# Linear attention feeding a mixture of experts: the rows of x prepared three blocks ahead, with four transposed buffers

## The chip, the cores and the metric

The kernel runs on one core of a Trainium2 chip. The metric is the time of one execution on the device in microseconds (us); lower is better. A run's time is a little longer than the span of its profile, which goes from the first to the last instruction that the profile shows.

## The reference, cut to what matters

```
q_s = softmax(q, axis=-1);  k_s = softmax(k, axis=2)            # q, k, v: 8 x 8 x 576 x 64
kv  = einsum('bhsd,bhse->bhde', k_s, v)
x   = einsum('bhsd,bhde->bhse', q_s, kv)  -> rows of 512         # 8 x 576 = 4608 rows
for b, s:
    fresh_e = argmax(x[b, s] @ w_gate)                           # 8 experts
    e = fresh_e if s == 0 or sigmoid(x[b, s] @ w_local) < 0.5 else prev_e
    p = softmax(x[b, s] @ w_gate)
    out[b, s] = p[e] * (relu(x[b, s] @ w1[e]) @ w2[e])           # w1: 512 x 1024, w2: 1024 x 512
```

Each of the 4608 rows of x goes to one expert, and which one hangs on the rows before it in its sequence.

## The kernel before, in words

The first part (up to about 150 us) works out the attention and writes the rows of x, not yet divided by their sums, to a buffer `xrows` in device memory. The rows are then sorted by expert into blocks of 128 rows, at most 43 of them (`NBM`), and each block is a pass through the two layers of one expert.

A block needs its rows prepared, in steps that stand on different engines:

- `gather` (line 828, POOL) fetches the 128 rows into one of four buffers `xg`.
- `prep_x` (`Px`, line 839, POOL, a few on VectorE) scales them by their sums into one of two buffers `xn`.
- `prep_hi` (`Ph`, line 184, ACT) writes the upper half of a split into two float16 numbers, and `prep_lo` (`Pl`, line 847, VectorE) the lower half, into one of two buffers `x2`. The trace calls these `x`.
- `turn_dma` (`D`, line 860, issued by SyncE) transposes both halves by DMA into one of three buffers `xT`.

Then TensorE runs `ffn1` (lines 882 and 887, half of the hidden units at a time, accumulators `ph` and `pi`); `act_copy`, `act_add`, `act_hi`, `act_lo` (lines 892, 895, 898, 902) add the two parts on ACT and VectorE, apply the relu and split the result into `hi` and `lo`; `ffn2` (line 909) multiplies by the second layer into the accumulator `py`; `give` (line 912, ACT) scales it by the row's share into one of two buffers `y`; and `put` (line 916, POOL) stores the rows by an indirect DMA. Since the stores go to rows that only the data name, each waits for the one before it.

All weights are split into float16 pairs too. `fetch` (line 976, SyncE, 2 MB each for w1 and for w2, into `s1` and `s2`) loads the next expert's weights, on a condition that is read at run time; `renew` (lines 184 and 938, ACT and VectorE) cuts them into `w1h`, `w1l`, `w2h`, `w2l` where a block begins a new expert.

Each engine works through its own list in order. For the first part and blocks 0 to 5 the order is a list written by hand, `ORDER`; a name such as `Px.6` is a step and a block. From block 6 on the order is that of the function `block(b)`:

```
        if b + AHEAD < NBM:
            gather(b + AHEAD)
        prep_a(b + 2)
        ...
        prep_b(b + 2)
        act(b, 1)
        ...
        ffn2(b, 0)
        ...
        if b + 2 < NBM:
            turn_dma(b + 2)
        fetch(b, 2)
        if b + 1 < NBM:
            fetch(b + 1, 1)
```

`prep_a` is `prep_x`, `prep_b` is `prep_hi` and `prep_lo`. TensorE's order in `block(b)` is `ffn1(b, 0)`, `ffn2(b - 1, 1)`, `ffn1(b, 1)`, `ffn2(b, 0)`. `AHEAD` is 4. Blocks 36 and up run only if the data need them. A block that is at most half full runs `ffn1` on 64 rows, so it is shorter.

Of the kernel before, what the change touches and what calls it, by code (L numbers as in the profile page):

```python
# [9 lines left out]
F16 = mybir.dt.float16  # L10
F32 = mybir.dt.float32
# [12 lines left out]
P = 128  # L24
# [117 lines left out]
bo.2 bo.0 Ar.3.0 bo.1 RN.3.3 Al.3.0 Gv.2 s2.3 bm.1 xs.3.2 bo.3 bm.0 Ac.3.1 ro.2.8 F2.3.0 ro.3.8 RN.4.1 Ad.3.1 Pt.2 ro.3.1 ro.3.6 bi.p0 F1.4.0 ro.3.7  # L142
Ar.3.1 s1.4 bi Sd.1 RN.4.2 Al.3.1 bj.p0 ro.3.3 F2.3.1 bj.p1 Ac.4.0 bj.p2 RN.5.0 ro.2.5 Ad.4.0 bm.3 Gv.3 bj.p3 bm.2 F1.4.1 Ar.4.0 bx.p0 RN.4.3 Al.4.0
bx bj.p4 F2.4.0 G.6 Ac.4.1 RN.5.1 Ad.4.1 G.7 Ar.4.1 bj F1.5.0 Al.4.1 s1.5 G.8 Gp.6 F2.4.1 Ac.5.0 Px.6 RN.6.0 Px.7 Ad.5.0 Ph.6 Ar.5.0 Pl.6 Ph.7 Al.5.0
F1.5.1 D.6 Gv.4 Pl.7 Pt.4 D.7 Pt.3 s2.4 RN.5.2 RN.5.3 F2.5.0 RN.6.1 s2.5 Ac.5.1 s1.6 G.9 Ad.5.1 Ar.5.1 Al.5.1
"""


# [1 line left out]
def moe_kernel(ctx, tc, q, k, v, w_gate, w_local, w1, w2, out, dbg=None):  # L150
# [433 lines left out]
    def r_o(t, c):  # L584

        o_ = oo[:, t * NCH + c, :]
        if on("ro", t, c) is nc.vector:
            nc.vector.tensor_scalar(out=o_, in0=iot1, scalar1=off[:, t, c:c + 1], scalar2=val[:, c:c + 1],
                                    op0=ALU.is_equal, op1=ALU.mult)
        else:  # L590
            da = sp.tile([P, P], F32, name="da")
            nc.scalar.activation(da, iot1, AF.Abs, bias=off[:, t, c:c + 1], scale=-1.0)
            nc.scalar.activation(o_, da, AF.Relu, bias=val[:, c:c + 1], scale=nval[:, c:c + 1])

# [195 lines left out]
    def open_w():  # L790

        ck.close()
        wp = ctx.enter_context(tc.tile_pool(name="wp", bufs=1, side="right"))
        for n, sh, dt in (("s1", [P, 4, DF], F32), ("s2", [P, 8, DM], F32), ("w1h", [P, 4, DF], F16),
                          ("w1l", [P, 4, DF], F16), ("w2h", [P, 8, DM], F16), ("w2l", [P, 8, DM], F16)):
            W[n] = wp.tile(sh, dt, name=n)
        fp = ctx.enter_context(tc.tile_pool(name="fp", bufs=1, side="right"))
        pst = ctx.enter_context(tc.tile_pool(name="pst", bufs=1, space=PSUM, side="right"))
        psy = ctx.enter_context(tc.tile_pool(name="psy", bufs=1, space=PSUM, side="right"))
        turns(fp, xg, AHEAD, [P, ROW], F32, "xg")  # L800
        turns(fp, xn, 2, [P, DM], F32, "xn")
        turns(fp, x2, 2, [P, 2, DM], F16, "x2")
        turns(fp, xT, 3, [P, 2, 4, P], F16, "xT")
        turns(fp, pb, NPB, [P, 1], F32, "pb")
        turns(pst, pt, 1, [P, 2, 4, P], F16, "pt")
        turns(psy, py, 1, [P, DM], F32, "py")
        psh = ctx.enter_context(tc.tile_pool(name="psh", bufs=1, space=PSUM, side="right"))
        fe = ctx.enter_context(tc.tile_pool(name="fe", bufs=1, side="right"))
        turns(fe, hi, 2, [P, 8, P], F16, "hi")
        turns(fe, lo, 2, [P, 8, P], F16, "lo")  # L810
        turns(fe, hf, 2, [P, 4, P], F32, "hf")
        turns(fe, ys, 2, [P, DM], F32, "y")
        turns(psh, ph, 1, [P, 4, 2 * P], F32, "ph")
# [40 lines left out]
                nc.tensor.transpose(pt[0][:, i, c, :], x2[b % 2][:, i, P * c:P * c + P], id16)  # L854

    def turn_copy(b):
        nc.vector.tensor_copy(out=xT[b % 3], in_=pt[0])

    def turn_dma(b):
        nc.sync.dma_start(out=xT[b % 3].rearrange("p i c t -> p (i c) t"), in_=x2[b % 2].rearrange("p i d -> p (i d)"),  # L860
                          transpose=True)

    def ffn1(b, g):
# [9 lines left out]

    def hidden(b, g, n):

        ph_, xT_ = ph[g % len(ph)], xT[b % 3]
        phs[g] = ph_
        for f in range(4):
            fs = slice(P * (4 * g + f), P * (4 * g + f) + P)

            def big(c):
                nc.tensor.matmul(ph_[:, f, :].rearrange("p (i t) -> p i t", i=2)[:, :, 0:n], W["w1h"][:, c, fs], xT_[:, :, c, 0:n],  # L882
                                 start=(c == 0), stop=(c == 3))

            big(0)
            for c in range(4):
                nc.tensor.matmul(ph_[:, f, 0:n], W["w1l"][:, c, fs], xT_[:, 0, c, 0:n], start=False, stop=False)  # L887
            for c in range(1, 4):
                big(c)
# [74 lines left out]
    def fetch(b, i):  # L964
# [8 lines left out]
        elif b == NA - 2 and i == 2:  # L973
# [2 lines left out]
        nc.sync.dma_start(out=s_, in_=src(bass.ds(word(e, NE - 1, [ET.SP]), 1)), **kw)  # L976

    pl = Plan(dict(kt=NKT, vt=NVT, km=2, mt=2, vp=2, pk=2, psq=2, px=1, pz=1, qt=NQT, qs=3, qe=4, xt=NXT, kvT=2, rs=3, cs=1,
                   qm=3, ex=2, xg=AHEAD, xn=2, x2=2, xT=3, pst=1, psh=1, psy=1, hh=2, hf=2, y=2, dl=1, pb=NPB),
              ("kt", "vt", "vp", "km", "xg", "xn", "x2", "xT", "pst", "psh", "hh", "hf", "y", "pb"), names(SWAP))  # L980
    add, split = pl.add, pl.split
    plan.append(pl)
# [86 lines left out]
    for b in range(NP + 4):  # L1069
        add(("G", b), POOL, gather, after=[("ax",) if b < NA else ("bx",)] + [("xs", t, u) for t in range(2 if b < NA else NTILE) for u in range(3)],  # L1070
            order=[("ow",)], takes=[("xg", b)])
        if b <= NP:
            add(("Gp", b), POOL, gather_share, after=[("ax",) if b < NA else ("bx",)] + [("Sd", t) for t in range(1 if b < NA else 2)],
                order=[("ow",)], takes=[("pb", b)])
        if b >= NP + 2:
            continue
        add(("Px", b), POOL, prep_x, alt=DVE, after=[("G", b)], uses=[("xg", b)], takes=[("xn", b)])
        add(("Ph", b), ACT, prep_hi, alt=DVE, after=[("Px", b)], uses=[("xn", b)], takes=[("x2", b)])
        add(("Pl", b), DVE, prep_lo, after=[("Ph", b)], uses=[("xn", b), ("x2", b)])
        if b < NT_PE:  # L1080
            add(("T", b), PE, turn, after=[("Pl", b)], takes=[("pst", b)], uses=[("x2", b)])
            add(("Tc", b), DVE, turn_copy, after=[("T", b)], uses=[("pst", b)], takes=[("xT", b)])
        else:
            add(("D", b), SP, turn_dma, after=[("Pl", b)], uses=[("x2", b)], takes=[("xT", b)])
        if b > NP:
            continue
        if b > 0:
            for i in range(2 if b == NP else 4):
                src = [("F1", b - 1, 0), ("F1", b - 1, 1), ("F2", b - 1, 0), ("F2", b - 1, 1)][i]
                add(("RN", b, i), ACT, renew4, after=[src, ("aj",) if b < NA else ("bj",)], order=[("s1" if i < 2 else "s2", b - 1)])  # L1090
            add(("s1", b), SP, lambda b: fetch(b, 1), after=[("RN", b, 1)] + ([("bj",)] if b >= NA - 1 else []))
        else:
            add(("s1", b), SP, lambda b: fetch(b, 1), after=[("Wl", i) for i in range(8)] + [("aj",)], order=[("W", 3)])
        if b == NP:
            continue
        add(("s2", b), SP, lambda b: fetch(b, 2),
            after=([("RN", b, 3)] if b else [("Wl", i) for i in range(8, 16)] + [("aj",)]) + ([("bj",)] if b >= NA - 2 else []))
        for g in range(2):
            wp_ = [("Wl", 4 * g + i) for i in range(4)] if b == 0 else [("RN", b, g)]
            add(("F1", b, g), PE, ffn1, after=[("Tc" if b < NT_PE else "D", b)] + wp_, order=[("ow",)] + ([("F2", b - 1, g)] if b else [("F1", 0, 0)] * g)  # L1100
                + ([("F1", b, 0)] if g else []), takes=[("psh", (b, g))], uses=[("xT", b)])
            add(("Ac", b, g), ACT, act_copy, after=[("F1", b, g)], uses=[("psh", (b, g))], takes=[("hf", (b, g))])
            add(("Ad", b, g), DVE, act_add, after=[("Ac", b, g)], uses=[("psh", (b, g)), ("hf", (b, g))])
            add(("Ar", b, g), ACT, act_hi, after=[("Ad", b, g)], uses=[("hf", (b, g))] + ([("hh", b)] if g else []), takes=[] if g else [("hh", b)])
            add(("Al", b, g), DVE, act_lo, after=[("Ar", b, g)], uses=[("hf", (b, g)), ("hh", b)])
            if b == NP - 1 and g:
                continue
            wp_ = [("Wl", 8 + 4 * g + i) for i in range(4)] if b == 0 else [("RN", b, 2 + g)]
            add(("F2", b, g), PE, ffn2, after=[("Al", b, g)] + wp_, order=[("F1", b, 1)] if g == 0 else [("F1", b + 1, 0)],
                takes=[] if g else [("psy", b)], uses=[("hh", b)] + ([("psy", b)] if g else []))  # L1110
        if b < NP - 1:
            add(("Gv", b), ACT, give, after=[("F2", b, 1), ("Gp", b)], uses=[("psy", b), ("pb", b)], takes=[("y", b)])
            add(("Pt", b), POOL, put, after=[("Gv", b)], uses=[("y", b)])
# [21 lines left out]
    def block(b):  # L1135


        if b + AHEAD < NBM:
            gather(b + AHEAD)
        prep_a(b + 2)  # L1140
        if b + 1 < NBM:
            gather_share(b + 1)
            if b + 1 not in fst:
# [8 lines left out]
        put(b - 1)  # L1152
        renew(b, FROM[b][1])
        next_(b, (2, 3))
        prep_b(b + 2)
        act(b, 1)
        renew(b, FROM[b][2])
        next_(b, (4, 5, 6, 7))
        ffn2(b, 0)
        next_(b, (8, 9))  # L1160
        if b + 2 < NBM:
            turn_dma(b + 2)
        fetch(b, 2)
        if b + 1 < NBM:
            fetch(b + 1, 1)
# [53 lines left out]
```

## Time and profile before

| what | before |
|---|---|
| median of three runs | 603.48 us (602.3, 603.48, 604.54) |
| the profiled execution's own time | 598.04 us |
| its span | 596.3 us |
| TensorE matmul busy | 516.5 us, 87% of the span |
| VectorE, ACT, POOL busy | 58%, 45%, 36% |
| mean granted clock of TensorE | 0.937 |

In a timeline row the first number is the start in us from the span's start, the second the duration; a merged row (x4) runs from the first start to the last end. A bracket names the idle time before the row and what ended it. The granted clock is a share of 2.4 GHz: 1.00 is full, 0.50 is 1.2 GHz. A row of the DMA view gives the number of issues and the median time from issue to landing.

### The profile page before, as it was taken

The numbers are of one execution on the slowest core, as the hardware profiler recorded it, in microseconds if no ns is written. First come the engines' busy times: TensorE is split into PE (matmuls) and PEld (weight loads), VectorE is DVE, ScalarE is ACT, GpSimd is POOL, SyncE is SP. The second block draws the span as 40 slices with busy tenths as digits, with TensorE's granted clock in tenths as the row PEclk, the third lists the DMA queues.
The fourth block names the chain that finished last, engine by engine and source line by source line (L and its number), as shares of the span: only waits on it lengthen the run. The fifth ranks groups of instructions, "written<-read, shape, count | busy, mean of one in ns | idle before, by whom it ended". The sixth has DMA issues, their size and how long they took to land. (4 is left out here: it accounts for less than half of the span.)

```text
span 596.3 us, 15110 instructions
## 1 busy us (share of the span) xinstructions
PE 516.5 (87%) x5558; PEld 366.1 (61%) x5558; DVE 348.8 (58%) x625; ACT 265.4 (45%) x441; POOL 213.9 (36%) x229
## 2 busy tenths in 40 slices
PE   2687966776589999799979999999999899999995
PEld 1566755554476776466656666667665666667762
DVE  3777789999978984227624853584376233333332
ACT  0534345395465533237424743564375243342432
POOL 4132323224613104623522533534434335243341
PEclk9768799777889999899989999999999999999998
DMA  9999999997855428633992596369539924333241
GB/s 238 245 240 214 259 251 263 263 211 192 287 201 143 117 83 255 241 74 96 287 128 58 158 259 85 100 199 208 111 61 286 157 58 104 68 90 83 69 103 47
DMA packets 100241, 98.29 MB, mean 165 GB/s; under 512 B 55199, under 2 KB 83871, under 8 KB 100128
## 3 DMA queue, kind: packets, MB, share of 16 engines
q1 hardware_dynamic: 92480, 74.66, 52.6%
q0 software_dynamic: 7648, 22.20, 13.4%
q8 instruction: 62, 1.02, 0.8%
q14 instruction: 51, 0.42, 0.3%
HBM read 206.76 MB, written 20.89 MB: 382 GB/s over the span
## 5 line engine op out<-in xcount | busy, mean ns | idle before, releaser
L909 PE MATMUL py<-w2h,hi 128*128 128x512 f16 x304 | 116.0, 382 | 8.2 <-ACTq L954 3.7
L916 POOL DMA_INDIRECT out<-y,sidx x38 | 39.2, 1032 | 217.8 <-ACTq L954 155.2
L909 PE MATMUL py<-w2h,lo 128*128 128x512 f16 x304 | 115.8, 381 | 0.6
L909 PE MATMUL py<-w2l,hi 128*128 128x512 f16 x304 | 115.8, 381 | 0.1
L882 PEld LDWEIGHTS <-w1h 128*128 128x128 f16 x1216 | 104.9, 99 | 14.6
L887 PEld LDWEIGHTS <-w1l 128*128 128x128 f16 x1216 | 92.3, 99 | 22.8 <-issue 6.0
L882 PE MATMUL ph<-xT,w1h 128*128 128x256 f16 (+1 forms) x624 | 99.1, 273 | 7.9 <-DMA xT<-x 7.9
L909 PEld LDWEIGHTS <-hi 128*128 128x128 f16 x608 | 58.8, 98 | 66.2 <-issue 9.7
L882 PE MATMUL pi<-xT,w1h 128*128 128x256 f16 (+1 forms) x592 | 91.7, 268 | 0.0
L902 DVE SCALAR_TENSOR_TENSOR lo<-hf,hi 128x512 f16<-128x512 f32 x76 | 56.9, 749 | 46.1 <-ACTq L954 38.9
L898 ACT ACTIVATE hi<-hf 128x512 f16<-128x512 f32 x76 | 47.8, 629 | 70.1 <-DVE hf L895 69.3
L895 DVE TENSOR_TENSOR hf<-ph,hf 128x512 f32<-128x512 f32 x39 | 26.9, 689 | 84.3 <-ACT hf L892 81.6
L892 ACT COPY hf<-ph 128x512 f32<-128x512 f32 x39 | 22.7, 582 | 97.6 <-PE ph L882 94.2
L847 DVE SCALAR_TENSOR_TENSOR x<-xn,x 128x512 f16<-128x512 f32 x40 | 33.7, 845 | 46.8 <-ACT x L184 45.7
L887 PE MATMUL ph<-xT,w1l 128*128 128x128 f16 (+1 forms) x624 | 60.5, 221 | 0.0
L887 PE MATMUL pi<-xT,w1l 128*128 128x128 f16 (+1 forms) x592 | 55.9, 217 | 0.0
L828 POOL DMA_INDIRECT xg<-xrows,gidx x42 | 44.6, 1062 | 30.2 <-issue 11.4
L909 PEld LDWEIGHTS <-lo 128*128 128x128 f16 x304 | 29.9, 98 | 39.1 <-DVE lo L902 2.5
L834 POOL DMA_INDIRECT pb<-shares,gidx x39 | 45.7, 1171 | 10.2 <-issue 6.8
L357 PE MATMUL pk<-VP,KT 128*64 128x65 f32 (+1 forms) x640 | 41.1, 286 | 4.0 <-POOL VP L186 1.9
L357 PEld LDWEIGHTS pk<-VP,KT 128*64 128x64 f32 (+1 forms) x640 | 33.5, 185 | 12.5 <-issue 4.7
L410 POOL TENSOR_TENSOR qs<-qt,qm 128x512 f32<-128x512 f32 x23 | 24.8, 1092 | 42.1 <-DVE qm L404 21.0
(223 smaller groups left out, 667.4 us busy)
## 6 DMA issues: line engine op xcount, KB each, us to landing
s<-in_moe_w SPq DMA_DIRECT2D x77, 2048.0 KB
xrows<-xt SPq DMA_DIRECT2D x12, 888.0 KB
qt<-in_q SPq DMA_DIRECT2D x24, 384.0 KB
KT<-in_k SPq DMA_DIRECT2D x16, 512.0 KB
VT<-in_v SPq DMA_DIRECT2D x16, 512.0 KB
s<-in_moe_w SPq DMA_DIRECT2D x4, 1024.0 KB
KT<-in_k SPq DMA_DIRECT2D x8, 128.0 KB
VT<-in_v SPq DMA_DIRECT2D x8, 128.0 KB
```

Of the source, the lines that this page charges most:

```text
L357: nc.tensor.matmul(pkv[64 * i:64 * i + 64, g], KT[b % NKT][ps, 4 * i + g, c], VP[b % 2][ps, 4 * i + g, c], start=(c == 0), stop=(c == KC - 1))
L410: on("qs", t, c).tensor_tensor(out=qs[t, c].rearrange("p (g x) d -> p g x d", x=2), in0=qt[t, c // 3][:, :, c % 3, :].rearrange("p (x g) d ...
L828: nc.gpsimd.indirect_dma_start(out=xg[b % AHEAD], out_offset=None, in_=src, in_offset=bass.IndirectOffsetOnAxis(ap=i_[:, j_:j_ + 1], axis=0))
L834: nc.gpsimd.indirect_dma_start(out=pb[b % NPB], out_offset=None, in_=src, in_offset=bass.IndirectOffsetOnAxis(ap=i_[:, j_:j_ + 1], axis=0))
L847: nc.vector.scalar_tensor_tensor(out=x2[b % 2][:, 1, :], in0=xn[b % 2], scalar=XS, in1=x2[b % 2][:, 0, :], op0=ALU.mult, op1=ALU.subtract)
L882: nc.tensor.matmul(ph_[:, f, :].rearrange("p (i t) -> p i t", i=2)[:, :, 0:n], W["w1h"][:, c, fs], xT_[:, :, c, 0:n], start=(c == 0), stop ...
L887: nc.tensor.matmul(ph_[:, f, 0:n], W["w1l"][:, c, fs], xT_[:, 0, c, 0:n], start=False, stop=False)
L895: nc.vector.tensor_tensor(out=hf[g], in0=phs[g][:, :, 0:P], in1=hf[g], op=ALU.add)
L898: nc.scalar.activation(hi[b % 2][:, 4 * g:4 * g + 4, :], hf[g], AF.Relu)
L902: nc.vector.scalar_tensor_tensor(out=lo[b % 2][:, gs_, :], in0=hf[g], scalar=0.0, in1=hi[b % 2][:, gs_, :], op0=ALU.max, op1=ALU.subtract)
L909: nc.tensor.matmul(py[0], h_[:, f, :], w_[:, f, :], start=(f == 0 and i == 0), stop=(f == 7 and i == 2))
L916: nc.gpsimd.indirect_dma_start(out=outr, out_offset=bass.IndirectOffsetOnAxis(ap=i_[:, j_:j_ + 1], axis=0), in_=ys[b % 2], in_offset=None, ...
```

## The change

The functions of the loop prepare block b+3 where they prepared block b+2. The transposed rows get a fourth buffer. Since the loop now starts with block 9, the preparation of block 8 (`Px.8 Ph.8 Pl.8`, `D.8`) is added to the written order. A scratch tile `da` of the sorting step goes from three buffers to two.

```diff
 bx bj.p4 F2.4.0 G.6 Ac.4.1 RN.5.1 Ad.4.1 G.7 Ar.4.1 bj F1.5.0 Al.4.1 s1.5 G.8 Gp.6 F2.4.1 Ac.5.0 Px.6 RN.6.0 Px.7 Ad.5.0 Ph.6 Ar.5.0 Pl.6 Ph.7 Al.5.0
-F1.5.1 D.6 Gv.4 Pl.7 Pt.4 D.7 Pt.3 s2.4 RN.5.2 RN.5.3 F2.5.0 RN.6.1 s2.5 Ac.5.1 s1.6 G.9 Ad.5.1 Ar.5.1 Al.5.1
+F1.5.1 D.6 Gv.4 Pl.7 Px.8 Ph.8 Pl.8 Pt.4 D.7 D.8 Pt.3 s2.4 RN.5.2 RN.5.3 F2.5.0 RN.6.1 s2.5 Ac.5.1 s1.6 G.9 Ad.5.1 Ar.5.1 Al.5.1
...
-            da = sp.tile([P, P], F32, name="da")
+            da = sp.tile([P, P], F32, name="da", bufs=2)
...
-        turns(fp, xT, 3, [P, 2, 4, P], F16, "xT")
+        turns(fp, xT, 4, [P, 2, 4, P], F16, "xT")
...
-        nc.sync.dma_start(out=xT[b % 3].rearrange("p i c t -> p (i c) t"), in_=x2[b % 2].rearrange("p i d -> p (i d)"),
+        nc.sync.dma_start(out=xT[b % 4].rearrange("p i c t -> p (i c) t"), in_=x2[b % 2].rearrange("p i d -> p (i d)"),
                           transpose=True)
...
-        ph_, xT_ = ph[g % len(ph)], xT[b % 3]
+        ph_, xT_ = ph[g % len(ph)], xT[b % 4]
...
-        if b >= NP + 2:
+        if b >= NP + 3:
             continue
...
-        prep_a(b + 2)
+        prep_a(b + 3)
...
-        prep_b(b + 2)
+        prep_b(b + 3)
         act(b, 1)
...
-        if b + 2 < NBM:
-            turn_dma(b + 2)
+        if b + 3 < NBM:
+            turn_dma(b + 3)
         fetch(b, 2)
```

How the lists of two engines change where the loop begins: POOL first. `xg` is a gather, `xn` the scaling, `pb` the gather of the shares, `out` the store. Before:

```order
L834 DMA pb_1707<-shares,gidx_76 128x1
L839 TENSOR_TENSOR xn_1699<-xg_1697 128x512
L954 UNCONDITIONAL_BRANCH
L916 DMA out<-y_1723,sidx_73 4608x512
L916 DMA out<-y_1724,sidx_73 4608x512
L828 DMA xg_1695<-xrows,gidx_76 128x592
L954 UNCONDITIONAL_BRANCH x3
L828 DMA xg_1696<-xrows,gidx_76 128x592
L839 TENSOR_TENSOR xn_1698<-xg_1694 128x512
L834 DMA pb_1708<-shares,gidx_76 128x1
```

After:

```order
L834 DMA pb_1708<-shares,gidx_76 128x1
L839 TENSOR_TENSOR xn_1699<-xg_1697 128x512
L954 UNCONDITIONAL_BRANCH
L839 TENSOR_TENSOR xn_1698<-xg_1694 128x512
L916 DMA out<-y_1724,sidx_73 4608x512
L916 DMA out<-y_1725,sidx_73 4608x512
L828 DMA xg_1695<-xrows,gidx_76 128x592
L828 DMA xg_1696<-xrows,gidx_76 128x592
L839 TENSOR_TENSOR xn_1699<-xg_1695 128x512
L834 DMA pb_1709<-shares,gidx_76 128x1
```

The fourth row of the new list is the scaling of block 8; it now stands ahead of the stores of blocks 4 and 3. Where block 8 was scaled (next to last row of the old list), block 9 is, whose gather is the one two rows above it, with one gather between.

SyncE's list at the same place, from the transpose of block 6 to the first weight fetch (`s`) behind it. Before:

```order
L860 DMA_TRANSPOSE xT_1702<-x_1700 128x8x128
L860 DMA_TRANSPOSE xT_1703<-x_1701 128x8x128
L822 TENSOR_LOAD info_74 x2
L976 REGISTER_ALU x2
L976 ISA
L976 DMA s_1680<-in_moe_w 128x8x512
```

After:

```order
L860 DMA_TRANSPOSE xT_1704<-x_1700 128x8x128
L860 DMA_TRANSPOSE xT_1705<-x_1701 128x8x128
L860 DMA_TRANSPOSE xT_1702<-x_1700 128x8x128
L822 TENSOR_LOAD info_74 x2
L976 REGISTER_ALU x2
L976 ISA
L976 DMA s_1680<-in_moe_w 128x8x512
```

The transpose of block 8 stands between that of block 7 and the weight fetch.

## Rows read from the trace of the kernel before

**Rows 1.** page, part 1: busy us (share of the span) x instructions
```profile
PE 516.5 (87%) x5558; PEld 366.1 (61%) x5558; DVE 348.8 (58%) x625; ACT 265.4 (45%) x441; POOL 213.9 (36%) x229
```

**Rows 2.** stretches: us, busy us (x) of each engine, granted clock, DMA share, GB/s
```profile
309.60:313.90 4.30, 4.28 (x32) 3.60 (x32) 0.00 (x0) 0.00 (x0) 0.00 (x0) 0.60 0.41 112
...
500.00:580.00 80.00, 80.00 (x688) 55.71 (x686) 26.99 (x39) 28.94 (x47) 32.64 (x32) 1.00 0.37 85
```

**Rows 3.** waits of TensorE: line waited for, us in total, times, longest us
```profile
PE ph L882 <- DMA xT<-x: 7.9, 4, 3.2
```

**Rows 4.** timeline of TensorE: start us, us, instruction, [idle before <-releaser]
```profile
237.55 0.27 PE L882 MATMUL ph<-xT,w1h 128*128 128x256 f16 x1
...
248.62 0.58 PE L909 MATMUL py<-w2h,hi 128*128 128x512 f16 x1 [3.04 <-ACTq L954]
...
305.99 0.38 PE L909 MATMUL py<-w2h,lo 128*128 128x512 f16 x1
309.62 0.32 PE L882 MATMUL ph<-xT,w1h 128*128 128x256 f16 x1 [3.25 <-DMA xT<-x]
...
313.91 0.38 PE L909 MATMUL py<-w2h,hi 128*128 128x512 f16 x1
...
316.50 0.27 PE L882 MATMUL pi<-xT,w1h 128*128 128x256 f16 x1
...
319.14 0.38 PE L909 MATMUL py<-w2h,hi 128*128 128x512 f16 x1
...
365.01 0.27 PE L882 MATMUL ph<-xT,w1h 128*128 128x256 f16 x1 [1.33 <-DMA xT<-x]
```

**Rows 5.** timeline of SyncE's queue, before the loop and around the longest wait
```profile
231.52 4.80 SPq L860 DMA_TRANSPOSE xT<-x  x2
238.41 13.59 SPq L976 DMA_DIRECT2D s<-in_moe_w  x3
...
286.39 2.26 SPq L860 DMA_TRANSPOSE xT<-x  x1
289.99 1.53 SPq L976 DMA_DIRECT2D s<-in_moe_w  x2
294.68 3.76 SPq L860 DMA_TRANSPOSE xT<-x  x1
...
304.77 1.27 SPq L860 DMA_TRANSPOSE xT<-x  x1
```

**Rows 6.** timeline of ACT, block 6 and around the longest wait
```profile
247.88 0.69 ACT L912 ACTIVATE y<-py,pb 128x512 f32<-128x512 f32 x1 [5.46 <-DMA xg<-xrows,gidx]
...
317.81 0.63 ACT L184 ACTIVATE x<-xn 128x512 f16<-128x512 f32 x1 [0.42 <-ACTq L954]
...
328.60 0.61 ACT L184 ACTIVATE x<-xn 128x512 f16<-128x512 f32 x1
```

**Rows 7.** DMA issues at 351.75, at 240.73, of the whole span: median us to landing
```profile
xg<-xrows,gidx POOLq DMA_INDIRECT x1, 13.0
...
out<-y,sidx POOLq DMA_INDIRECT x1, 7.1
...
out<-y,sidx POOLq DMA_INDIRECT x38, 3.1
```

**Rows 8.** timeline of POOL, before the loop and in it
```profile
232.59 1.04 POOL L839 TENSOR_TENSOR xn<-xg 128x512 f32<-128x512 f32 x1 [3.79 <-DMA xg<-xrows,gidx]
235.14 1.02 POOL L916 DMA_INDIRECT out<-y,sidx  x1 [1.52 <-ACTq L954]
240.73 1.00 POOL L916 DMA_INDIRECT out<-y,sidx  x1 [4.56 <-DMA out<-y,sidx]
...
320.03 1.06 POOL L839 TENSOR_TENSOR xn<-xg 128x512 f32<-128x512 f32 x1
...
351.75 1.02 POOL L828 DMA_INDIRECT xg<-xrows,gidx  x1 [0.30 <-issue]
...
363.14 1.06 POOL L839 TENSOR_TENSOR xn<-xg 128x512 f32<-128x512 f32 x1
```

More of the change, by code (lines that the diff above doesn't have):

```diff
@@ L856, in turn_copy @@
     def turn_copy(b):
-        nc.vector.tensor_copy(out=xT[b % 3], in_=pt[0])
+        nc.vector.tensor_copy(out=xT[b % 4], in_=pt[0])
     def turn_dma(b):
-        nc.sync.dma_start(out=xT[b % 3].rearrange("p i c t -> p (i c) t"), in_=x2[b % 2].rearrange("p i d -> p (i d)"),
+        nc.sync.dma_start(out=xT[b % 4].rearrange("p i c t -> p (i c) t"), in_=x2[b % 2].rearrange("p i d -> p (i d)"),
                           transpose=True)
@@ L978, in moe_kernel @@
     pl = Plan(dict(kt=NKT, vt=NVT, km=2, mt=2, vp=2, pk=2, psq=2, px=1, pz=1, qt=NQT, qs=3, qe=4, xt=NXT, kvT=2, rs=3, cs=1,
-                   qm=3, ex=2, xg=AHEAD, xn=2, x2=2, xT=3, pst=1, psh=1, psy=1, hh=2, hf=2, y=2, dl=1, pb=NPB),
+                   qm=3, ex=2, xg=AHEAD, xn=2, x2=2, xT=4, pst=1, psh=1, psy=1, hh=2, hf=2, y=2, dl=1, pb=NPB),
               ("kt", "vt", "vp", "km", "xg", "xn", "x2", "xT", "pst", "psh", "hh", "hf", "y", "pb"), names(SWAP))
```

## The prediction

> **What bounds the kernel now.** I read the page first, then TensorE's waits, then its timeline around each long wait, then the queues that feed it. TensorE is busy for 516.5 of 596.3 us [rows 1], and in the stretch from 500 to 580 us it is never idle and its granted clock is 1.00 [rows 2]. So in the loop over blocks only what makes TensorE wait, or lowers its clock, can be won. The list of waits holds one entry that the change aims at: the first products of a block waited four times for the transposed rows, 7.9 us together, the longest 3.2 us [rows 3].
>
> The timeline shows what such a wait costs. The last second-layer matmul starts at 305.99 and the next block's first product at 309.62 [rows 4]. That group of first products then lasts 313.91 - 309.62 = 4.29 us, while an undisturbed one lasts 319.14 - 316.50 = 2.64 us [rows 4]: the granted clock was 0.60 in the stretch behind the wait [rows 2], a mean between the two levels. So this wait has a tail of 1.65 us. The wait at 365.01 (1.33 us) is followed by matmuls at full pace, as the others of its size are; I give the tail to the longest alone.
>
> Why are the rows late? SyncE issues the transposes in a fixed order with the weight fetches. Around the longest wait it issued a transpose at 286.39, a weight fetch at 289.99, a transpose at 294.68 and the next at 304.77 [rows 5]. The block that waited until 309.62 reads what was issued at 294.68, one block and a bit before: 14.9 us from issue to use, behind a weight fetch. The transpose of 286.39, ahead of that fetch, held nobody up.
>
> **The change part by part.**
> *Three blocks ahead.* In the loop each of the steps (product on POOL, copy on ACT, subtraction on VectorE, transpose on SyncE) keeps its place and works for block b+3 instead of b+2. Each block so finds its rows issued one slot earlier. For the four waiting blocks that slot lies 8.3 us before (286.39 instead of 294.68 [rows 5]), more than twice the longest wait of 3.2 us [rows 3]. All four go: 7.9 us, and the tail of 1.65 us. The wait is counted from the modelled end of the last matmul, 0.38 us after its start, while matmuls start every 0.216 us when nothing holds them (twelve between 313.91 and 316.50 [rows 4]); so 4 x 0.16 = 0.6 us more. Gain 10.2 us.
>
> *What is late next in the loop.* (a) Only two buffers hold the split rows. The copy on ACT for block b+3 overwrites those of b+1, whose transpose must have read them; until now it overwrote those of b, whose transposed rows TensorE was already using. At the longest wait that transpose would land 309.62 - 305.99 = 3.6 us into the block at the latest; the copy stands at 317.81 [rows 6], 8.2 us behind 309.62, or 6.5 without the slow clock. Cover 2.9 us, so nothing is paid. (b) The product on POOL now needs the gather issued one round before, not two. The slowest gather I found was issued at 351.75 and took 13.0 us, to 364.7 [rows 7]; the product one round on stands at 363.14 [rows 8]. POOL would wait 1.6 us. Behind it in POOL's queue stand the gather of the shares and the next store, whose result waits for later work. ACT takes such a product 7.5 us after it ends (320.03 + 1.06 to 328.60 [rows 6, 8]), so this too is hidden. In the first round of the loop only one gather lies between a block's gather and its product (block 9, POOL's list above); if it takes the 7.1 us of a store issued there [rows 7], the product ends near 250, ACT's copy comes about 2 us later than before, and the result behind it is used by TensorE half a block later still. (c) The transposes and fetches keep their places on SyncE. Zero.
>
> *The preparation added before the loop.* Block 8 is now prepared in the written order, ahead of POOL's stores of blocks 4 and 3, ahead of TensorE's last first-layer result on ACT and VectorE, and its transpose stands on SyncE ahead of three weight fetches. POOL's product: the one for block 7 ends at 232.59 + 1.04 = 233.6, the store of block 4 starts at 235.14 [rows 8], so 1.06 us fits between if the gather has landed. ACT: the copy needs the transpose of block 6 (issued at 231.52) to have read its buffer; that has landed by 237.55, when TensorE starts block 6 without a wait [rows 4, 5]. I take 235.5 for the copy, then 236.2 for the subtraction, each some 0.65 us; what stands behind them on both engines is used at 240 us or later and absorbs 1.2 us.
>
> SyncE: the transpose can be issued at about 236.9 and takes 1.25 us, so the weight fetch of 238.41 [rows 5] moves back by about 1.8 us. No weights are due then. But TensorE waits 3.04 us at 248.62 for its accumulator, which ACT empties at 247.88 [rows 4, 6], and ACT waits there for the output buffer that the store of block 3 reads (the row names a gather, which ACT does not read; the store's landing is what falls on that time): issued at 240.73 and 7.1 us under way, to 247.8, against a median of 3.1 us [rows 7, 8]. That store was stuck behind the fetch. **If the fetch moves by 1.8 us, I let the store, ACT and TensorE move by 1.8 us.** The lower bound: the store slips ahead of the later fetch, takes its median, and the wait goes: 3.04 + 0.16 us, with a tail like the other's of 1.65, a gain of 4.9. The upper bound: the copy starts as late as 237.55, 2.1 us more than I took, and the shift is 3.9 us. I take 1.8, nearer to the row, because the fetch would still start ahead of most of the store's packets.
>
> The Trainium skill has a rule against this last term: DMA: Bandwidth & Descriptors, Queues, rings and completion order, says that each DMA engine takes turns between the queues that have work, packet by packet, so a store on POOL's queue would share with SyncE's fetch rather than stand behind it. By that rule the term would be about zero and the sum 593.3. The row of 7.1 us against 3.1 speaks for more than sharing, and I stay with it.
>
> *Edits at no cost.* The scratch tile on ACT drops from three buffers to two; both its writer and its reader are on ACT, in order. The fourth buffer of transposed rows is memory alone. At the end one block more is prepared in vain, beside TensorE's last blocks.
>
> **Sum.** -10.2 + 1.8 = -8.4 us. On the profiled execution's own 598.04 us (596.3 of span, 1.7 around it) that gives 589.6. The median of the three runs is 603.48, 5.4 us above the profiled one; the same saving taken from it gives **595.1 us**. That the unprofiled runs wait as often is an assumption.
>
> **The rivals.**
> *The wait only moves (13%).* With two split buffers, ACT would stand at its copy for the transpose of block b+1 and hold back the results behind it. It decides where the transpose lands later than 6.5 us into the block before its own; the longest now lands at 3.6. If fetch and gathers together make it 3 us later in those four blocks, they give back about 4 x 2 us, and the time is 603.48 - 8.4 + 8 = 603.1.
> *The gather is too slow for its new distance (8%).* POOL's product waits for a gather issued one round before. It decides where a gather takes longer than the 11.4 us from 351.75 to 363.14 plus the product and the 7.5 us to ACT's copy, some 19 us. Against it: the slowest is 13.0. For it: the transposes behind a fetch already take 15. If the four fetches drive it to 22 us, ACT stands 3 us each time, with a tail of 1.65 us on TensorE: 4 x 4.65 = 18.6, so 603.48 - 8.4 + 18.6 = 613.7, slower than before.
> *The change does not do what it says (5%).* If the rows were late because SyncE issues late, not because they land late, a slot earlier would change little. Against it: the transpose of 294.68 was issued long before its use. Then only the cost remains: 603.48 + 1.8 = 605.3.
> *No cost, by the sharing of queues (14%).* The 593.3 us above, worked out from rows as a term of zero.
>
> **How the numbers follow.** My forecast has 60%; with the last rival 74% on the faster side. The low end takes the gain at 10.2 plus 4.9: 603.48 - 15.1 = 588.4, so 588. The high end takes the upper cost of 3.9 and most of the first rival, as far as 602.5. What a measurement tells from no change is 0.5%, 3 us. Faster by more: 74%. Within it: the first rival and the third, 18%. Slower: the second, 8%.
>
> **What the profile would show.** Right: no wait of first products on transposed rows; the block around the first long wait keeps a granted clock of 1.00; ACT's copy of split rows waits for no DMA; SyncE's fetch before the loop some 2 us later and TensorE's wait for the accumulator at block 6 some 5 us. Wrong: waits of ACT on the copy, of POOL's product for gathers of more than 7 us, or TensorE still waiting for transposed rows.

## The result, and the profile after

The changed kernel takes 595.33 us (median of 20 runs, 591.02 to 601.65) against 601.03 us for the kernel before (20 runs, 596.95 to 609.91). The ratio is 0.9907, with a 95% interval from 0.9885 to 0.9929; it is formed without the runs that lie over 1.5% above the fastest of their kernel, so it can differ from the ratio of the medians, here and below. Measured once more later on, the same two kernels stood at 596.11 and 600.05 us, ratio 0.9963 [0.9925, 1.0001], whose interval just reaches 1. By the medians it is faster by 5.7 us in the first measurement and by 3.9 in the second; by the ratios it is 5.6 and 2.2. The profiled execution took 594.43 us.

The stretches of the changed kernel, from the start of block 5's second first-layer half to block 7, and from block 7 to the end; columns as in [rows 2]:

```profile
236.90:258.60 21.70, 18.82 (x133) 11.69 (x132) 6.31 (x9) 6.29 (x11) 8.20 (x8) 0.84 0.80 232
258.60:592.50 333.90, 322.06 (x2741) 218.99 (x2739) 155.41 (x222) 149.35 (x253) 136.24 (x127) 1.00 0.58 131
```

The same two stretches of the kernel before:

```profile
231.60:252.70 21.10, 17.55 (x133) 11.25 (x132) 6.27 (x9) 6.05 (x10) 10.41 (x11) 0.92 0.75 243
252.70:596.30 343.60, 324.19 (x2741) 220.08 (x2739) 155.47 (x220) 148.57 (x251) 132.24 (x123) 0.99 0.54 126
```

From block 7 to the end it is 9.7 us shorter with the same 2741 records of matmuls, and the granted clock there is now 1.00, before 0.99. In this execution the part ahead of it happened to be 5.3 us longer (236.90 against 231.60), so the whole spans differ by 3.7 us only; that part is taken up under the experiments.

TensorE's waits in the changed kernel (columns as in [rows 3]):

```profile
PE py L909 <- ACT y L912: 3.5, 4, 1.4
...
PE py L909 <- ACTq L954: 2.7, 1, 2.7
```

The line of [rows 3], first products that wait for transposed rows, is not in the list any more. The 3.5 us on `y` were there before, in the same number and length. What is left of the transition is one wait of 2.7 us, and it stands at another place than the 3.04 us of [rows 4]. TensorE's timeline:

```profile
239.21 0.49 PE L882 MATMUL pi<-xT,w1h 128*128 128x256 f16 x3
242.44 0.59 PE L909 MATMUL py<-w2h,hi 128*128 128x512 f16 x1 [2.73 <-ACTq L954]
...
247.82 0.42 PE L882 MATMUL ph<-xT,w1h 128*128 128x256 f16 x1
...
255.71 0.49 PE L882 MATMUL pi<-xT,w1h 128*128 128x256 f16 x3
256.04 0.38 PE L909 MATMUL py<-w2h,hi 128*128 128x512 f16 x1
```

The wait is now at the second layer of block 5. In the kernel before, TensorE waited a fifth of that at this place:

```profile
234.96 0.38 PE L909 MATMUL py<-w2h,hi 128*128 128x512 f16 x1 [0.51 <-ACTq L954]
```

The twelve matmuls behind the wait last 247.82 - 242.44 = 5.38 us, where an undisturbed dozen takes 2.6 [rows 4]: half the pace. Block 6 (256.04), where TensorE waited 3.04 us before, goes on without a gap. What ACT did there:

```profile
240.05 0.67 ACT L912 ACTIVATE y<-py,pb 128x512 f32<-128x512 f32 x1
241.71 0.63 ACT L184 ACTIVATE x<-xn 128x512 f16<-128x512 f32 x1 [0.99 <-DMA xT<-x]
242.92 0.58 ACT L892 COPY hf<-pi 128x512 f32<-128x512 f32 x1 [0.58 <-ACTq L954]
...
255.30 0.69 ACT L912 ACTIVATE y<-py,pb 128x512 f32<-128x512 f32 x1 [2.26 <-DMA out<-y,sidx]
257.64 0.63 ACT L184 ACTIVATE x<-xn 128x512 f16<-128x512 f32 x1 [1.65 <-POOL xn L839]
```

The row at 241.71 is the added copy for block 8 (`Ph.8`). It waits 0.99 us until the transpose of block 6 has read its buffer, ends at 242.34, and behind it ACT comes to the run-time branch of `RN.5.2` (the `ACTq L954` that TensorE waits for), the next step on its list. SyncE's queue and POOL's timeline at the same place:

```profile
237.50 7.58 SPq L860 DMA_TRANSPOSE xT<-x  x3
246.61 13.90 SPq L976 DMA_DIRECT2D s<-in_moe_w  x3
```

```profile
238.44 1.04 POOL L839 TENSOR_TENSOR xn<-xg 128x512 f32<-128x512 f32 x1 [4.05 <-DMA xg<-xrows,gidx]
240.00 1.04 POOL L839 TENSOR_TENSOR xn<-xg 128x512 f32<-128x512 f32 x1 [0.52 <-DMA xg<-xrows,gidx]
...
246.63 1.00 POOL L916 DMA_INDIRECT out<-y,sidx  x1 [4.14 <-DMA out<-y,sidx]
...
256.56 1.04 POOL L839 TENSOR_TENSOR xn<-xg 128x512 f32<-128x512 f32 x1 [6.38 <-DMA xg<-xrows,gidx]
```

Counted from the start of block 5's second first-layer half, the weight fetch goes out at 246.61 - 236.90 = 9.7 us, before at 238.41 - 231.65 = 6.8: 2.95 us later. The store of block 3 (246.63) is issued in the same moment as the fetch and lands at about 255.3, where ACT's wait ends: 8.7 us, read from that wait, against a median of 3.1 [rows 7].

### The profile page after: what moved, and what is told of

Same layout as the page of the kernel before. It is cut to its first block, busy times and chain, and to the rows that moved or that the text cites. A ratio compares the mean times of both kernels' runs of the same rounds, so it can differ in the third digit from the quotient of the medians.

```text
span 592.6 us, 15086 instructions
## 1 busy us (share of the span) xinstructions
PE 522.8 (88%) x5558; PEld 371.2 (63%) x5558; DVE 349.1 (59%) x626; ACT 266.2 (45%) x442; POOL 213.1 (36%) x230
## 5 line engine op out<-in xcount | busy, mean ns | idle before, releaser
L882 PE MATMUL ph<-xT,w1h 128*128 128x256 f16 (+1 forms) x624 | 97.7, 270 | 0.0
L902 DVE SCALAR_TENSOR_TENSOR lo<-hf,hi 128x512 f16<-128x512 f32 x76 | 54.8, 721 | 46.1 <-ACTq L954 37.6
L847 DVE SCALAR_TENSOR_TENSOR x<-xn,x 128x512 f16<-128x512 f32 x41 | 35.0, 857 | 45.1 <-ACT x L184 43.5
L834 POOL DMA_INDIRECT pb<-shares,gidx x39 | 43.5, 1116 | 7.9 <-issue 7.6
L839 POOL TENSOR_TENSOR xn<-xg 128x512 f32<-128x512 f32 x35 | 37.3, 1067 | 16.7 <-DMA xg<-xrows,gidx 12.6
L357 PE MATMUL pk<-VP,KT 128*64 128x65 f32 (+1 forms) x640 | 39.9, 280 | 2.7 <-issue 1.9
```

The source lines that it names most:

```text
L357: nc.tensor.matmul(pkv[64 * i:64 * i + 64, g], KT[b % NKT][ps, 4 * i + g, c], VP[b % 2][ps, 4 * i + g, c], start=(c == 0), stop=(c == KC - 1))
L834: nc.gpsimd.indirect_dma_start(out=pb[b % NPB], out_offset=None, in_=src, in_offset=bass.IndirectOffsetOnAxis(ap=i_[:, j_:j_ + 1], axis=0))
L839: eng.tensor_tensor(out=xn[b % 2].rearrange("p (g x d) -> p g x d", g=4, x=2), in0=xg[b % AHEAD].rearrange("p (g x) -> p g x", g=4)[:, :, ...
L847: nc.vector.scalar_tensor_tensor(out=x2[b % 2][:, 1, :], in0=xn[b % 2], scalar=XS, in1=x2[b % 2][:, 0, :], op0=ALU.mult, op1=ALU.subtract)
L902: nc.vector.scalar_tensor_tensor(out=lo[b % 2][:, gs_, :], in0=hf[g], scalar=0.0, in1=hi[b % 2][:, gs_, :], op0=ALU.max, op1=ALU.subtract)
```

## The experiments

Two quantities are read from each kernel's timeline of TensorE, since they don't depend on how long the first part took. The *stretch* goes from the start of block 5's second first-layer half to the first product of block 7, the *loop* from there to the end of the span. The third number is what TensorE waited for transposed rows in the loop.

| kernel | first part | stretch | loop | waits on xT | stretch + loop |
|---|---|---|---|---|---|
| before | 231.6 | 21.1 | 343.6 | 7.9 (4) | 364.7 |
| before, once more | 230.2 | 19.5 | 341.2 | 6.0 (3) | 360.8 |
| e1: `da` alone | 230.6 | 21.2 | 343.4 | 6.4 (3) | 364.6 |
| e2: four buffers, two ahead | 230.9 | 19.2 | 337.0 | 3.8 (3) | 356.2 |
| e6: two ahead, store of 3 early | 236.4 | 16.4 | 343.8 | 8.2 (3) | 360.2 |
| after | 236.9 | 21.7 | 333.9 | none | 355.6 |
| after, once more | 236.6 | 21.8 | 334.2 | none | 356.0 |
| e4: three buffers, three ahead | 227.7 | 22.6 | 334.0 | none | 356.6 |
| e8: three ahead, store of 3 early | 229.0 | 19.8 | 333.5 | none | 353.3 |
| e5: block 8 prepared later | 231.2 | 19.1 | 335.7 | none | 354.8 |
| e7: e5 and the store early | 233.4 | 16.2 | 335.8 | none | 352.0 |
| e9: e7, product before gather | 241.1 | 16.6 | 340.6 | none | 357.2 |

The first part spreads from 227.7 to 241.1 us. Both profiles of the changed kernel were long there, but e8, which up to block 5 differs only in the place of one store, took 229.0. I take that for spread between executions; it wasn't tested. There is a rival. The profiles of e1 to e8 and the second one of the kernel before come from one chip, on which the kernel before took 594.53 and 593.13 us, and those of e9 and of the repeat of the changed kernel from another, on which it took 600.05; for the first pair the chip isn't known. So the first part may hang on the chip. The loop doesn't show it: the repeat has 334.2 us there, the changed kernel's like on the first chip 333.5 and 334.0.

Every kernel below was also timed. Single runs of one kernel lie 2% and more apart, so intervals of 0.4% around a ratio don't order kernels that differ by 1 to 3 us. The stages are read for that, but each row is one profile, and the four rows of the same order (before, its repeat, e1, e2) run from 356.2 to 364.7 us in stretch and loop. Of the nine ratios forecast below, only those of e1 and e4 came out in their range; the other seven came out above it, slower than forecast.

**The distance and the buffer, apart.** The scratch tile alone, on the kernel before:

```diff
-            da = sp.tile([P, P], F32, name="da")
+            da = sp.tile([P, P], F32, name="da", bufs=2)
```

> The kernel before with the scratch tile da at two buffers, nothing else. My theory: writer and reader are both on ACT in order, so the time stays: within 0.3% of before (ratio 0.997 to 1.003). The rival, to explain why the changed kernel gained 5.6 us where its loop shows a gain of 9: this edit costs 2 to 4 us in the sorting step or before it (ratio 1.003 to 1.007), seen as a later start of block 6 in the trace.

Measured 595.36 us against 594.53, ratio 0.9999 [0.9962, 1.0037]. It costs nothing. With the fourth buffer besides, still two blocks ahead:

```diff
-        turns(fp, xT, 3, [P, 2, 4, P], F16, "xT")
+        turns(fp, xT, 4, [P, 2, 4, P], F16, "xT")
...
-        nc.vector.tensor_copy(out=xT[b % 3], in_=pt[0])
+        nc.vector.tensor_copy(out=xT[b % 4], in_=pt[0])
```

and so in the two other places that name `xT[b % 3]`.

> The kernel before with four transposed buffers and da at two, but still prepared two blocks ahead. My theory: the gain is the distance, so nothing moves: ratio 0.997 to 1.003, and TensorE still waits for transposed rows four times, some 8 us. The rival: a buffer more, or where the tiles lie, is what helps: ratio about 0.99 and fewer waits.

Measured 596.53 against 594.53 us, ratio 1.0059 [1.0014, 1.0104]: no gain. The profiled execution, 588.84 us, was the shortest of its twelve, so its short loop and its three waits of 3.8 us in place of the expected 8 are no sign of one. Then the other half, the changed kernel with three buffers, and `xT[b % 3]` throughout:

```diff
-        turns(fp, xT, 4, [P, 2, 4, P], F16, "xT")
+        turns(fp, xT, 3, [P, 2, 4, P], F16, "xT")
```

> The changed kernel, three blocks ahead, but with three transposed buffers: the transpose for block b+3 writes where block b's rows lie and is issued behind that block's last first-layer product. My theory: SyncE comes to that transpose after this product is done anyway or waits for it by less than 1 us, so the time is that of the changed kernel, some 5 to 6 us below before (ratio 0.988 to 0.993) and no wait for transposed rows. The rival: the fourth buffer is needed, the transpose is held until the product ends, the weight fetch behind it too, and half of the gain or more goes (ratio 0.995 to 1.0), with waits for transposed rows back in the list.

Measured 588.16 against 594.53 us, ratio 0.9905 [0.9872, 0.9938]. TensorE's waits on transposed rows, of the second profile of the kernel before:

```profile
PE ph L882 <- DMA xT<-x: 6.0, 3, 2.9
```

of e2:

```profile
PE ph L882 <- DMA xT<-x: 3.8, 3, 1.9
```

and what e4 has in the same list for the second layer, with no line for transposed rows:

```profile
PE py L909 <- ACTq L954: 4.6, 2, 2.7
...
PE py L909 <- ACT y L912: 3.5, 4, 1.4
```

Distance alone takes the waits away and gives as large a gain as the whole change (0.9905 against 0.9907); the fourth buffer alone leaves three of them, and beside the distance it isn't needed. The rival by which a slot earlier changes little falls too. The distance moves four steps at once, from POOL's product to SyncE's transpose; which of them had to come earlier isn't separated.

**How large the waits are.** One more profile of the kernel before:

> The kernel before once more, for its profile. My theory: how long its loop waits for transposed rows differs between executions; from the start of block 7 to the end I expect 337 to 344 us, with 4 to 8 us of waits, against 334 in the changed kernel. The rival: the loop always takes 343 to 344 us, and what the unprofiled runs lack of the forecast was lost ahead of the loop.

It took 592.75 us, with three waits of 6.0 us together. Over the five kernels that prepare two ahead, the waits run from 3.8 to 8.2 us, mean 6.5, and the loop from 337.0 to 343.8, mean 341.8. The profile on which the prediction rests had the second longest waits. The changed kernel, its repeat, e4 and e8 have 333.5 to 334.2, mean 333.9. **The loop gains 7.9 us in the mean.** One thing more stands in the five traces: all 16 waits come 17 to 20 us behind a weight fetch whose issue takes 0.4 us on SyncE's queue (for the longest, the first of the two at 289.99 in [rows 5]), while most other issues of a fetch take under 0.1 us, presumably because the condition skips the transfer. That fits the prediction's reason, rows behind a fetch. No experiment moves such a fetch, so the reason stays argued; shown is that rows prepared one block earlier don't come late.

**The cost before the loop.** Block 8 is prepared behind block 5's steps:

```diff
-F1.5.1 D.6 Gv.4 Pl.7 Px.8 Ph.8 Pl.8 Pt.4 D.7 D.8 Pt.3 s2.4 RN.5.2 RN.5.3 F2.5.0 RN.6.1 s2.5 Ac.5.1 s1.6 G.9 Ad.5.1 Ar.5.1 Al.5.1
+F1.5.1 D.6 Gv.4 Pl.7 Pt.4 D.7 Pt.3 s2.4 RN.5.2 RN.5.3 F2.5.0 RN.6.1 s2.5 Ac.5.1 s1.6 Px.8 G.9 Ad.5.1 Ar.5.1 Al.5.1 Ph.8 Pl.8 D.8
```

> The changed kernel with block 8's preparation moved back in the written order: its product behind the store of block 3, its copy and subtraction behind block 5's last results, its transpose behind the three weight fetches. My theory: at block 5's second layer TensorE waits for ACT, which stood behind the copy of block 8; here that wait falls from 2.7 us to about 0.5, the store of block 3 lands some 2 us sooner, but the wait of about 3 us for the accumulator at block 6 with its slow clock comes back, so the time is 0.5 to 1 us below the changed kernel (ratio to before 0.986 to 0.992). The rival: the place of the preparation costs what the loop's gain lost, 3 us: ratio 0.982 to 0.986.

Measured 590.41 against 594.53 us, ratio 0.9968 [0.9922, 1.0013]. The wait at block 5 falls from 2.73 to 0.66 us, and the 3.04 us at block 6 come back as 2.48; the stretch is 19.1 us. So the added preparation is what TensorE waits for; that it is the copy on ACT in it is read from ACT's rows above. But the loop is 1.8 us longer. A wait that takes 0.39 us in the changed kernel (at 287.97) takes 1.96 here:

```profile
281.22 0.38 PE L909 MATMUL py<-w2h,hi 128*128 128x512 f16 x1 [1.96 <-ACT y L912]
```

Then the store of block 3 goes ahead of the gathers and the fetch, first in the kernel before:

```diff
-bx bj.p4 F2.4.0 G.6 Ac.4.1 RN.5.1 Ad.4.1 G.7 Ar.4.1 bj F1.5.0 Al.4.1 s1.5 G.8 Gp.6 F2.4.1 Ac.5.0 Px.6 RN.6.0 Px.7 Ad.5.0 Ph.6 Ar.5.0 Pl.6 Ph.7 Al.5.0
-F1.5.1 D.6 Gv.4 Pl.7 Pt.4 D.7 Pt.3 s2.4 RN.5.2 RN.5.3 F2.5.0 RN.6.1 s2.5 Ac.5.1 s1.6 G.9 Ad.5.1 Ar.5.1 Al.5.1
+bx bj.p4 F2.4.0 Pt.3 G.6 Ac.4.1 RN.5.1 Ad.4.1 G.7 Ar.4.1 bj F1.5.0 Al.4.1 s1.5 G.8 Gp.6 F2.4.1 Ac.5.0 Px.6 RN.6.0 Px.7 Ad.5.0 Ph.6 Ar.5.0 Pl.6 Ph.7 Al.5.0
+F1.5.1 D.6 Gv.4 Pl.7 Pt.4 D.7 s2.4 RN.5.2 RN.5.3 F2.5.0 RN.6.1 s2.5 Ac.5.1 s1.6 G.9 Ad.5.1 Ar.5.1 Al.5.1
```

> The kernel before with the store of block 3 issued earlier on POOL, ahead of the gather of block 6, where POOL idles for 11 us; nothing else. My theory: at block 6 TensorE waits about 3 us because the output buffer is still read by that store, stuck behind a weight fetch; the wait and its slow clock go, so from the first-layer second half of block 5 to the start of block 7 it takes about 16.5 us instead of 21, and the time falls by 4 to 5 us (ratio 0.991 to 0.994). The rival: something else holds the accumulator's emptying there (flags, the share's gather) and the stretch stays at 21 us, the ratio within 0.996 to 1.004.

Measured 590.93 against 593.13 us, ratio 1.0005 [0.9946, 1.0063]. The 3.04 us wait is gone and the stretch falls to 16.4, from 20.2 in the mean of the four rows above it in the table. The time shows none of it, as the rival had it: the ratio is 1. The profile, of the longest of the twelve executions (598.30 us), has the longest waits on rows of all, 8.2 us, but whether the one brings the other isn't shown. What e6 does show is that the wait at block 6 hangs on when the store of block 3 goes out. Issued at 226.62, that store landed after 3.2 us; the next two, issued at 239.93 and 248.73 on either side of the fetch of 243.22, took 5.6 and 6.5. So stores near the fetch were slow here too. But transposes and gathers go on in the same stretch, and in the kernel before the store of block 3 also waited 4.56 us for the store ahead of it [rows 8]: that the fetch alone made it late isn't shown. The same edit with the late preparation, and with the preparation as it was changed:

> The changed kernel with block 8's preparation later, as in the run before of that kind, and the store of block 3 earlier. My theory: both waits around the start of the loop go, TensorE's stretch from the first-layer second half of block 5 to block 7 falls from 21.7 to about 16.5 us, and the four waits for transposed rows stay away: about 12 us below before (ratio 0.977 to 0.984). The rival: one of the waits is taken over by the next in line, and the ratio stays at about 0.988 to 0.992, as the changed kernel's.

> The changed kernel with the store of block 3 earlier, the preparation of block 8 left where it is. My theory: in the changed kernel TensorE stands for ACT at block 5's second layer, not for the store, so ACT's wait for the store of block 3 goes from its list but the stretch stays near 21 us and the time within 1.5 us of the changed kernel's (ratio 0.988 to 0.992). The rival: the store is still what counts and the stretch falls by 3 to 5 us (ratio 0.982 to 0.985).

e7: 587.26 against 593.13 us, 0.9943 [0.9901, 0.9985]; e8: 587.70 against the same 593.13, 0.9983 [0.9941, 1.0025]. The stretch is 16.2 and 19.8 us. In e8 the second layer of block 5 begins with these rows:

```profile
233.62 0.38 PE L909 MATMUL py<-w2h,hi 128*128 128x512 f16 x1 [1.83 <-ACTq L954]
234.36 0.58 PE L909 MATMUL py<-w2l,hi 128*128 128x512 f16 x1 [0.36 <-DVEq L954]
234.74 0.63 PE L909 MATMUL py<-w2h,lo 128*128 128x512 f16 x1
```

With the store out of the way, preparing block 8 early costs 19.8 - 16.2 = 3.6 us, all of it in the wait of 1.83 us, the second of 0.36 and the slow matmuls behind them. By the stages e7 is 3.6 us better than the changed kernel (352.0 against 355.6), by the medians 5.9 us better than the kernel before (3.4 by the ratio), where about 12 had been expected. That is a tie with the 5.7 of the change, so no version is shown to beat it. By its ratio alone e8 isn't told from the kernel before. Why the times show less than the stages stays open.

**The longer wait in e5 and e7.** VectorE's and POOL's rows in e7 at block 8:

```profile
269.26 1.97 DVE L847 SCALAR_TENSOR_TENSOR x<-xn,x 128x512 f16<-128x512 f32 x1
```

```profile
269.61 1.06 POOL L839 TENSOR_TENSOR xn<-xg 128x512 f32<-128x512 f32 x1
```

and in the changed kernel, where the subtraction is over before POOL's product begins:

```profile
278.04 0.69 DVE L847 SCALAR_TENSOR_TENSOR x<-xn,x 128x512 f16<-128x512 f32 x1
```

```profile
278.98 1.07 POOL L839 TENSOR_TENSOR xn<-xg 128x512 f32<-128x512 f32 x1
```

The subtraction takes 1.3 us more where the product runs beside it, and behind it VectorE, ACT and at 280.47 TensorE are late. The test moves the product ahead of the gather in e7:

```diff
-        if b + AHEAD < NBM:
-            gather(b + AHEAD)
         prep_a(b + 3)
+        if b + AHEAD < NBM:
+            gather(b + AHEAD)
```

> The kernel of the seventh experiment (late preparation, early store of block 3), and in each round of the loop POOL computes the product before it issues the gather, so about 1.1 us earlier. In six profiles the subtraction of the split (line 847) took 0.69 us wherever POOL's product did not overlap it, and 1.4 to 2.3 us wherever it did, in block 8 of the late kernels 1.97 us, after which TensorE waited 1.96 us on ACT near 281. If the overlap causes the length: the subtraction at block 8 overlaps the product by at most some 0.3 us and takes at most about 1.0 us, the wait near 281 falls from 1.96 to below 1.0 us, and the loop from block 7 on takes 334 to 335 us instead of 335.8. Rival: the length comes from elsewhere (the weight cuts beside it, ACT): the subtraction still takes about 2 us and the wait stays. By time the two can hardly be told apart (1 to 2 us of 588); ratio to before 0.985 to 0.995 either way.

Measured 596.32 against 600.05 us, ratio 0.9966 [0.9919, 1.0012]. The profiled execution took 600.19 us, at the upper end of its runs, so its instructions are read here rather than its total. VectorE and POOL in e9, at the same place:

```profile
276.20 2.35 DVE L938 SCALAR_TENSOR_TENSOR w1l<-s,w1h 128x512 f16<-128x512 f32 x2 [0.83 <-ACT w1h L184]
278.47 0.68 DVE L847 SCALAR_TENSOR_TENSOR x<-xn,x 128x512 f16<-128x512 f32 x1
```

```profile
276.33 1.06 POOL L839 TENSOR_TENSOR xn<-xg 128x512 f32<-128x512 f32 x1
```

The subtraction is down to 0.68 us, as the theory had it. But the product now meets the cut of weights in front of it: 2.35 us, where the same pair takes 1.29 in e7:

```profile
268.05 1.29 DVE L938 SCALAR_TENSOR_TENSOR w1l<-s,w1h 128x512 f16<-128x512 f32 x2 [0.83 <-ACT w1h L184]
```

The delay is 1.06 us, as long as POOL's product. TensorE's wait there is 1.74 us instead of 1.95, not below 1.0, and over the loop such waits grew:

```profile
288.40 0.38 PE L909 MATMUL py<-w2h,hi 128*128 128x512 f16 x1 [1.74 <-ACT y L912]
```

The whole loop of e9, and below it that of e7:

```profile
257.70:598.20 340.50, 325.03 (x2741) 219.88 (x2739) 178.19 (x221) 149.66 (x252) 134.45 (x125) 0.98 0.51 129
```

```profile
249.60:585.30 335.70, 321.86 (x2741) 218.86 (x2739) 156.65 (x220) 148.57 (x251) 131.94 (x125) 1.00 0.57 131
```

VectorE is busy 178.19 us instead of 156.65 with one instruction more: behind the gather's issue, in its old place, the product met 6 of the 35 subtractions from 225 us on, and now it meets 22. So it is shown that the overlap makes VectorE's instructions long. That this delay is what TensorE waits for fits (1.3 us lost in e7 and 1.06 in e9, waits of 1.95 and 1.74), but no run takes the delay away, so it isn't shown. In this one profile the loop is longer than that of e7; e7 wasn't timed beside e9, so the times don't compare them. TensorE's waits on `y` in e9, and below them those in e7, are

```profile
PE py L909 <- ACT y L912: 7.9, 4, 2.2
```

```profile
PE py L909 <- ACT y L912: 5.1, 4, 1.9
```

The other 2 us of the longer loop go with the lower granted clock (0.98), of which I can't say what brought it.

**The change once more.** No edit.

> The changed kernel once more, unaltered, on the chip and beside the runs of the experiment before it. If the gain of 5.6 us and the stages of its first profile hold: ratio to before 0.987 to 0.994, no wait of first products on transposed rows, block 7 to the end 333.5 to 334.5 us, the stretch before it 21 to 22.5 us with a wait of 2.0 to 3.0 us at the second layer of block 5. If the first profile's 2.73 us wait was an accident of that execution, the stretch is below 20 us.

Measured 596.11 against 600.05 us, ratio 0.9963 [0.9925, 1.0001]. The waits on transposed rows are absent again, the stretch has its waits at block 5 again (2.32 and 0.36 us, and 1.32 at block 6). They are no accident of the first profile.

## Why the prediction was right, and where it wasn't

- **Three blocks ahead takes the waits away: right**, shown by e4, which has the distance without the fourth buffer. The term was mis-sized: 10.2 us forecast, 7.9 in the mean of the profiles. "That the unprofiled runs wait as often is an assumption" was the weak place: the profile had four waits and 7.9 us, the mean is 6.5, and the other four profiles had three. In the pair of profiles first taken the loop did differ by 9.7.
- **The preparation added before the loop: right in size by luck, wrong in its path.** Forecast +1.8 us; the changed kernel, its repeat and e4 have a stretch of 22.0 us in the mean, the four kernels before in the same order 20.2, so +1.8. But the working said that what stands behind block 8's copy "absorbs 1.2 us". It doesn't: behind it stands the branch of `RN.5.2`, and TensorE waits 2.73 us there instead of 0.51, with twelve matmuls at half pace. The fetch moved by 2.95 us instead of 1.8: the copy had to wait for the transpose of block 6 and started 241.71 - 236.90 = 4.8 us into the stretch, where the working took 235.5 - 231.65 = 3.9, and the transpose of block 8, behind it, stood at the end of the 7.58 us of SyncE's three. TensorE came so late to block 6 that its 3.04 us were gone. In e4 it came sooner (a wait of 1.88 us at block 5), and 2.70 us at block 6 were back. Two errors of opposite sign met. The tail that the forecast expected behind the wait at block 6 stands at block 5.
- **The rival by sharing of queues** had the store slip past the fetch at no cost. The store of block 3 took 8.7 us beside the fetch, and in e6 and e8, where it is issued earlier, TensorE's wait at block 6 is gone. The prediction's reading that ACT waited there for this store, and not for the gather that the row names, is borne out by that. The rule of the Trainium skill (DMA: Bandwidth & Descriptors, Queues, rings and completion order) that queues take turns is not refuted by this, but here turns were not enough to keep the store near its 3.1 us.
- **The gathers: right.** POOL waited for them longer than before, and the long one came where it was forecast, in the first round of the loop (256.56, after 6.38 us). The lists for POOL, before and after:

```profile
POOL xn L839 <- DMA xg<-xrows,gidx: 3.8, 1, 3.8
```

```profile
POOL xn L839 <- DMA xg<-xrows,gidx: 12.6, 5, 6.4
```

  ACT's copy waited 1.65 us for the last of them (257.64), and TensorE not at all.
- **Two buffers of split rows: right in the loop.** ACT's copy waited for a transpose once, the 0.99 us at 241.71, and that is ahead of the loop. The rival in which the wait only moves to ACT came true there, for one block.
- **The edits at no cost: right** (e1, e4).
- **The sum.** Forecast -8.4 us; the stages give -7.9 + 1.8 = -6.1, the medians -5.7 and -3.9, the ratios -5.6 and -2.2. The time of 595.1 came out so near to 595.33 because the median it was taken from, 603.48, is 2.45 us above the one of 20 runs. The direction and the mechanism in the loop were earned; the cost ahead of it and the last digit were luck.

## What to carry to other kernels

A late operand wants distance in the order of issue. Here another buffer without it bought nothing, and the distance fitted in the buffers that were there. A step added to an in-order list must be followed on every engine to the next thing that another engine waits for: here TensorE waited for a branch right behind it, where the forecast had looked for the cost in a DMA queue. And waits that depend on when transfers land are a sample: take two or three profiles before their sum becomes a term.

## What the runs showed of the hardware that I had not expected

In six profiles (before, its repeat, after, e4, e5, e7) the subtraction of line 847 took 0.68 to 0.75 us in all 179 cases from 225 us on in which POOL's product did not overlap it, and 1.39 to 2.26 us in all 29 in which it did; POOL's product stayed between 1.04 and 1.07 us in these 29. e9 moved the overlap to another VectorE instruction, and the length went with it (1.29 to 2.35 us). The Trainium skill (SBUF — State Buffer, Who interferes with whom) says that a VectorE instruction with two inputs in SBUF contends with a GpSimd instruction that reads SBUF, and that the order of issue decides which of the two blocks. The 29 cases agree with the contention. They don't show the order: in 27 of them the subtraction started first, as in e7 (269.26 against 269.61), and in all 29 it was the one that took longer. Nor is the loss always one product: it is 1.06 us in e9, but the longest subtractions lost 1.57 (2.26 - 0.69).

The second is the pace behind a wait. The 2.73 us at block 5 were followed by a dozen matmuls at half pace (granted clock 0.84 over the stretch), while in e4 a wait of 1.88 and one of 0.36 us at the same place were followed by matmuls every 0.22 us, at full pace. In e8 1.83 and 0.36 us at that place were followed by matmuls every 0.43 us at first. The rows of e4, to be set beside those of e8 above:

```profile
232.34 0.38 PE L909 MATMUL py<-w2h,hi 128*128 128x512 f16 x1 [1.88 <-ACTq L954]
233.08 0.38 PE L909 MATMUL py<-w2l,hi 128*128 128x512 f16 x1 [0.36 <-DVEq L954]
233.29 0.38 PE L909 MATMUL py<-w2h,lo 128*128 128x512 f16 x1
```

The same kernel shows it too. Behind the 3.04 us at block 6 [rows 4] the dozen took 252.70 - 248.62 = 4.08 us in the first profile of the kernel before; in its second, the wait was no shorter and the dozen took 249.75 - 247.16 = 2.59:

```profile
247.16 0.38 PE L909 MATMUL py<-w2h,hi 128*128 128x512 f16 x1 [3.13 <-ACTq L954]
...
249.75 0.27 PE L882 MATMUL ph<-xT,w1h 128*128 128x256 f16 x1
```

So the length of the wait alone does not tell what follows it, and a tail read behind one wait, as the prediction took it, need not stand behind the next.
